# Frequency products rebuilt: sums by accumulating DMAs, mirrored inverse rows, the last W4 groups behind the inverse, and the order as written lists

## The chip, the cores and the metric

One core of a Trainium2 chip runs the kernel. The metric is device time in microseconds (us) of one execution, the median of several runs on the chip. TensorE does the matmuls, ScalarE (ACT) moves results out of PSUM and does the nonlinear functions, VectorE (DVE) does elementwise work in SBUF, GpSimd (POOL) issues some DMAs and does a few tiny operations, SyncE (SP) issues most DMAs.

## The reference

Two branches on the same input `x` (2048 rows, 640 columns, bfloat16), mixed by a gate per row:

```python
x = A_q
g = sigmoid((x * gate_w).sum(-1, keepdims=True))
return g * A(x, A_k, A_v, ...) + (1 - g) * B(x, B_w1, B_w2, B_w3, B_w4)

def A(q, k, v, shift_k, ssm_k, ssm_D):        # long convolution
    k_shift = sum of 4 shifted k, each times a row of shift_k
    kv = k_shift * v
    y = irfft(rfft(pad(kv)) * rfft(pad(ssm_k)))[:2048]     # along the rows, per column
    return q * (y + kv * ssm_D)

def B(x, w1, w2, w3, w4):                     # mixer and MLP
    h = gelu(layernorm(x) @ w1);  hs = (four column groups shifted by 1, -1, 2, -2 rows) @ w2
    x1 = x + hs
    return x1 + gelu(layernorm(x1) @ w3) @ w4
```

## The kernel before

**The operations as nodes.** The Python program makes a list of nodes, one for an engine's operation, with what each reads and writes. `Prog._forward` (from line 210) then plans an order from estimated costs and priorities (`RANK`), and `emit` writes one instruction stream for each engine in that order, with semaphore waits between engines. Each engine works through its stream strictly in order. PSUM is four pairs of banks; a group of matmuls (a job) takes a pair, and the evictions on ScalarE give it back.

**Branch B.** Rows are held as two halves `c` and eight residues `rho` (row = 1024 c + 8 p + rho on partition p). `mm1`, `mm2` (L1075), `mm3` (L1129) and `mm4` (L1147) are its four matmuls. `mm4` goes in four groups `sc` of four row sets; a group's PSUM is first filled with `x1` by ScalarE (`seed`, L1057), then 24 matmuls of 320 columns are added, and one eviction writes the result times `1 - g` back to `X`. All four groups come ahead of the convolution's products in the program; the planner spreads them over the time that VectorE needs.

**Branch A.** The convolution's transform is split: 16 row residues are combined by matmuls with tables of cosines (`forward`, L1178) for two frequency sets `kap` = 0 and 1, on two halves of the columns, for both signals: `h` (the filter taps) and `k` (k times v). Each result, 16 planes of 320 columns, lies in a slot `s0` to `s4`, `t0`, `t1` (or `k0`, `k1`: a column half of `KV`, rows of 640 bytes). For each of the four (half, kap) `unit` then works on VectorE alone, nearly everything through the helper `tt` (L663):
- `butterfly` of `h` and `k`: two instructions of 2560 elements (lower planes plus and minus upper planes) and four of 1280;
- `window`: two of 1280 on `k`;
- `pointwise`: the complex products, six multiplications of 2560, two sums (the first, `pwa`, is an accumulating DMA issued on POOL by `add_dma`, L702; the second is VectorE's) and two last ones (`pwz`);
- `fold`: the way back, two of 2560 and four of 1280.

`inverse` (L1366) makes for each residue `rho` 8 matmuls of 320 columns from both frequency sets; ScalarE evicts them times `g`, VectorE multiplies by q, and adds to `X`: for half 0 by accumulating DMAs (L1392), for half 1 on VectorE, row by row. The last four residues of half 1 are cut into pieces (L1341, L1351) and end the kernel.

**Order around the change.** SP's queue carries the loads, the transposes of the second layer norm, q and the stores; POOL's carries the loads of W3, W4 and the inverse table, the accumulating DMAs and the power instruction of the layer norms (L868).

Of the kernel before, what the change touches and what calls it, by code (L numbers as in the profile page):

```python
# [88 lines left out]
class Prog:  # L89
    LAT = {"pe": (0.0, 0.20), "act": (0.24, 0.16), "dve": (0.12, 0.12), "pool": (0.2, 0.2), "sp": (0.1, 0.1)}  # L90
    LOOK = 1.0

# [86 lines left out]
    PRIO = ()  # L179

    def schedule(self):
        for n in self.nodes:
            n.base = frozenset(n.deps)
        for j in self.jobs:
            own = set(j.nodes)
            j.ext = [d for v in j.nodes if not v.first for d in v.base if d not in own]
            if j.seeded:
                j.nodes[0].soft = [d for v in j.pes for d in v.base if d not in own]
        for n in self.nodes:
            for d in n.deps:  # L190
                d.users.append(n)
        for n in self.nodes:
            n.prio = self.PRIO[n.idx]
        self._forward()

    RATE = 390e3
    WINDOW = 3.4133
    PHASE = 2.4

    def _forward(self):  # L200
        nodes = self.nodes
        for n in nodes:
            n.deps = set(n.base)
            n.missing = len(n.deps)
            n.start = n.end = None
        for j in self.jobs:
            j.pair = None
            j.left = len(j.evicts) if j.evicts else 1
        free = {"pe": 1.0, "act": 0.7, "dve": 0.8, "pool": 1.1, "sp": 0.7}
        ready = {e: [] for e in ENGS}  # L210
        known_at = {}
        pair_free = [0.0] * PAIRS
        pair_job = [None] * PAIRS
        bits = [[False, False] for _ in range(PAIRS)]
        link = 0.0
        xlink = 0.0
        alink = 0.0
        slink = 0.0
        warm = False
        window = -1  # L220
        duty = carry = 0.0
        busy, lock = False, 0.0
        LAT = self.LAT

        def arrive(n):
            at = 0.0
            for d in n.deps:
                t = d.end + (LAT[d.eng][0 if d.eng == n.eng else 1] if d.kind == "c" else 0.05)
                if t > at:
                    at = t  # L230
            known_at[n] = at
            ready[n.eng].append(n)

        for n in nodes:
            if n.missing == 0:
                arrive(n)
        left = len(nodes)
        order = {e: [] for e in ENGS}
        allseq = []
        while left:  # L240
            best = None
            for e in ENGS:
                for n in ready[e]:
                    t = max(known_at[n], free[e])
                    if n.first:
                        j = n.job
                        tp = None
                        for i in range(PAIRS):
                            if pair_job[i] is not None and pair_job[i].left:
                                continue  # L250
                            if j.seeded and not (bits[i][0] and bits[i][1]):
                                continue
                            if tp is None or pair_free[i] < tp:
                                tp = pair_free[i]
                        if tp is None:
                            continue
                        t = max(t, tp)
                        ok = True
                        for d in j.ext:
                            if d.end is None:  # L260
                                ok = False
                                break
                            if not n.seed:
                                t = max(t, d.end - n.cost)
                        if ok and n.seed:
                            for d in n.soft:
                                if d.end is None:
                                    ok = False
                                    break
                                t = max(t, d.end - self.LOOK)  # L270
                        if not ok:
                            continue
                    key = (t, -n.prio, n.idx)
                    if best is None or key < best[0]:
                        best = (key, n)
            assert best is not None, "schedule is stuck"
            n = best[1]
            e = n.eng
            t = best[0][0]
            ready[e].remove(n)  # L280
            n.start = t
            cost = n.cost
            if n.array:
                w = int((t - self.PHASE) // self.WINDOW)
                while window < w:
                    warm = duty > (0.42 if warm else 0.75) * self.WINDOW
                    window += 1
                    duty, carry = carry, 0.0
# [225 lines left out]

def _tables():

# [929 lines left out]
```

## Time and profile before

| | |
|---|---|
| runs | median 225.89 us (225.49 to 226.24, three runs) |
| profiled execution | span 223.5 us from the first to the last instruction; its own time is not listed apart |
| TensorE busy | 216.3 us (97%), 1557 matmuls |
| VectorE busy | 208.7 us (93%), 267 instructions |
| ScalarE busy | 174.6 us (78%) |
| POOL busy | 41.1 us (18%), 48 instructions |
| DMA | 34.04 MB, mean 152 GB/s |

How to read it: spans and windows are in microseconds from the first instruction. A busy share is over the whole span; stages differ. A group row gives the line, engine, operation, shapes and count, then busy time and mean nanoseconds of one, then the idle time of the engine ahead of them with what ended it. A timeline row gives start, length and what ran, merged when the same thing follows itself. A window row gives for each engine its busy time and the number of its instructions, then the TensorE clock granted, the share of the DMA engines and GB/s.

### The profile page before, as it was taken

To read this page: it belongs to the slowest core of one execution; us is meant where nothing else is said; L and a number is where in the kernel's file an instruction comes from. 1 tells how busy PE (TensorE), PEld (TensorE's weight loads), DVE (VectorE), ACT (ScalarE), POOL (GpSimd) and SP (SyncE) were. 2 spreads that over 40 slices of the span, in tenths; PEclk is the share of its full clock that TensorE was granted. 3 is DMA by queue.
4 is the path that set the end of the run, shared out by engine and by line. 5 is a ranking of instruction groups with operands and counts; after the bars stand their busy time and mean duration, and the time that the engine had idled before them with its cause. 6 is when DMAs were issued, how large, how long until landed. Compare 5 with 4: busy or idle time off the path is not lost.

```text
span 223.5 us, 3945 instructions
## 1 busy us (share of the span) xinstructions
PE 216.3 (97%) x1557; PEld 138.0 (62%) x1569; DVE 208.7 (93%) x267; ACT 174.6 (78%) x292; POOL 41.1 (18%) x48
## 2 busy tenths in 40 slices
PE   7999999999999999999999999999999999999993
PEld 7589655557676655457744455667745675577772
DVE  4999899999999899999899999799998999999976
ACT  3989999899999999999987488997145723572484
POOL 1335662403003120450200200000020002033020
PEclk9999999999999999999999999999999999999999
DMA  6999996589801968061654150003559000648667
GB/s 208 385 403 387 350 361 236 116 156 283 349 5 33 345 120 337 4 117 41 126 101 90 24 97 0 1 3 98 137 87 257 11 0 3 117 87 117 151 117 235
DMA packets 36713, 34.04 MB, mean 152 GB/s; under 512 B 17508, under 2 KB 31719, under 8 KB 36568
## 3 DMA queue, kind: packets, MB, share of 16 engines
q1 hardware_dynamic: 31560, 23.97, 35.8%
q0 software_dynamic: 4848, 9.50, 18.9%
q10 hardware_dynamic: 288, 0.33, 0.6%
q8 instruction: 12, 0.20, 0.4%
q14 instruction: 5, 0.04, 0.1%
HBM read 21.47 MB, written 3.93 MB: 114 GB/s over the span
## 4 chain that ended last, share of the span: by engine, by line
PE 76%; ACT 18%; DVE 2%; DMA 2%; issue 1%; SPq 0%; ACTq 0%
PE PS L1147 23%; PE PS L1129 23%; ACT arena L694 12%; PE PS L1178 9%; PE PS L967 8%; PE PS L1366 6%; ACT PS L1057 5%; PE PS L927 2%; ACT arena L680 2%; DVE arena L663 2%; DMA arena<-in_A_q_dram 2%; PE PS L823 1%; PE PS L769 1%; PE PS L758 1%; PE PS L780 0%
## 5 line engine op out<-in xcount | busy, mean ns | idle before, releaser
L663 DVE TENSOR_TENSOR arena<-arena 128x2560 bf16<-128x2560 bf16 (+5 forms) x175 | 186.1, 1116 | 7.0 <-ACT arena L694 3.5
L694 ACT ACTIVATE arena<-PS 128x640 bf16<-128x640 f32 (+8 forms) x142 | 104.2, 812 | 18.9 <-PE PS L1129 14.7
L1147 PE MATMUL PS<-arena 128*128 128x320 bf16 x384 | 53.3, 299 | 0.0
L1129 PE MATMUL PS<-arena 128*128 128x512 bf16 x232 | 52.2, 379 | 0.8 <-ACT arena L694 0.5
L1147 PEld LDWEIGHTS PS<-arena 128*128 128x128 bf16 x384 | 37.4, 98 | 15.0 <-issue 0.3
L694 ACT ACTIVATE arena<-PS,arena 128x320 bf16<-128x320 f32 (+1 forms) x47 | 27.7, 626 | 24.2 <-PE PS L1147 22.2
L1129 PEld LDWEIGHTS PS<-arena 128*128 128x128 bf16 x240 | 23.3, 98 | 27.4 <-issue 0.5
L1178 PE MATMUL PS<-arena 128*128 128x320 bf16 x224 | 34.4, 300 | 0.7 <-DVE arena L906 0.6
L1178 PEld LDWEIGHTS PS<-arena 128*128 128x128 bf16 x224 | 20.8, 98 | 12.8 <-ACT arena L694 2.8
L680 ACT ACTIVATE arena<-arena 128x640 bf16<-128x640 bf16 (+2 forms) x34 | 25.8, 787 | 0.8 <-DMA arena<-in_A_q_dram 0.4
L967 PE MATMUL PS<-arena 128*128 128x512 bf16 (+1 forms) x121 | 22.9, 335 | 0.2
L1075 PE MATMUL PS<-arena 128*128 128x320 bf16 x160 | 22.6, 299 | 0.0
L1057 ACT ACTIVATE PS<-arena 128x640 f32<-128x640 bf16 x32 | 22.3, 719 | 0.2
L868 POOL TENSOR_TENSOR arena<-arena 128x4 f32<-128x4 f32 (+1 forms) x9 | 14.0, 1553 | 30.7 <-DVE arena L668 30.4
L1075 PEld LDWEIGHTS PS<-arena 128*128 128x128 bf16 x160 | 15.4, 98 | 6.7 <-ACT PS L1057 0.6
L967 PEld LDWEIGHTS PS<-arena 128*128 128x128 bf16 x125 | 11.8, 98 | 8.2 <-ACT arena L694 0.5
L702 POOL DMA_DIRECT2D arena<-arena x4 | 4.8, 1202 | 57.6 <-DVE arena L663 57.6
L888 DVE BATCH_NORM_STATS2 arena<-arena 128x6 f32<-128x320 bf16 x28 | 12.4, 477 | 2.9 <-DMA arena<-in_A_q_dram 2.8
L1366 PE MATMUL PS<-arena 128*128 128x320 bf16 x96 | 14.3, 299 | 0.0
L1007 POOL DMA_DIRECT2D arena<-arena x18 | 9.7, 545 | 12.7 <-ACT arena L694 12.7
L1366 PEld LDWEIGHTS PS<-arena 128*128 128x128 bf16 x96 | 9.2, 98 | 4.3 <-issue 0.3
L1392 POOL DMA_DIRECT2D arena<-arena x4 | 5.1, 1276 | 35.7 <-ACT arena L694 25.9
(42 smaller groups left out, 81.5 us busy)
## 6 DMA issues: line engine op xcount, KB each, us to landing
arena<-in_B_w_dram POOLq DMA_DIRECT2D x4, 960.0 KB, 8.2
arena<-in_A_k_dram SPq DMA_DIRECT2D x4, 640.0 KB, 14.3
arena<-in_A_v_dram SPq DMA_DIRECT2D x4, 640.0 KB, 14.1
arena<-arena POOLq DMA_DIRECT2D x4, 640.0 KB, 6.1
arena<-in_A_q_dram SPq DMA_DIRECT2D x4, 640.0 KB, 7.4
out_dram<-arena SPq DMA_DIRECT2D x15, 160.0 KB, 2.0
arena<-in_A_q_dram SPq DMA_DIRECT2D x6, 320.0 KB, 5.5
arena<-in_A_ssm_k_dram SPq DMA_DIRECT2D x3, 512.0 KB, 11.5
```

Of the source, the lines that this page charges most:

```text
L663: return dve(lambda e: e.tensor_tensor(o, a, b, op), [a, b], [o], c_tt(n), tag=tag, **kw)
L680: node = P.op("act", lambda e, ps: e.activation(o, i, func, **kw), r=r, w=[o], cost=c_act(n, naps, acc is not None, psum=False), tag=tag, ...
L694: node = P.op("act", lambda e, ps: e.activation(ov, inner(ps), func, **kw), r=r, w=[o], cost=c_act(n, len(r), acc is not None), job=job, t ...
L868: P.op("pool", lambda e, ps: e.tensor_tensor(r, v, hv, ALU.pow), r=[v, HALF], w=[r], cost=cost, tag="ln")
L888: dve(lambda e, o=o, x=x: e.bn_stats(o, x), [x], [o], 0.393, tag="bn", group=("bn", id(mv), rho, c))
L967: fns.append(lambda e, ps, b=b, c=c, lhsT=lhsT: e.matmul(bank(ps, b, 256 * n), lhsT, XT[:, c, r0:r0 + n, :], start=(c == 0), stop=(c == 4)))
L1057: P.seed(job, lambda e, ps: e.activation(two(ps, 320), x, ACTF.Copy), [X[:, c, rho, :]], c_act(640, psum=False), tag)
L1075: fns.append(lambda e, ps, hh=hh, ft=ft, lhsT=lhsT: e.matmul(bank(ps, hh, 320), lhsT, w2v[:, ft, 320 * hh:320 * hh + 320], start=False, st ...
L1129: fns.append(lambda e, ps, b=b, ft=ft, c=c, sc=sc: e.matmul(bank(ps, b, 512), w3h[ft // 6][:, c, 128 * (ft % 6):128 * (ft % 6) + 128], XT[ ...
L1147: fns.append(lambda e, ps, hh=hh, ft=ft, lhsT=lhsT: e.matmul(bank(ps, hh, 320), lhsT, w4h[ft // 6][:, ft % 6, 320 * hh:320 * hh + 320], st ...
L1178: fns.append(lambda e, ps, w=w, b=b, rhs=rhs, st=(first and n == 0), en=(n == len(ss) - 1): e.matmul(bank(ps, b, 320), w, rhs, start=st, s ...
L1366: fns.append(lambda e, ps, w=w, z=z, c=c, st=(n == 0), en=(n == len(terms) - 1): e.matmul(bank(ps, c, 320), w, z[:, c, :], start=st, stop=en))
```

## The change

The order is no longer planned at build time: `RANK` lists 993 ranks, one for each node, by which the nodes of all engines are sorted, and `PAIR` gives each job its PSUM pair. DMA semaphores are used again by later DMAs.

```diff
+    def schedule(self, rank, pairs):
+        for n in self.nodes:
+            n.prio = rank[n.idx]
+        self.allseq = sorted(self.nodes, key=lambda n: -n.prio)
+        self.order = {e: [n for n in self.allseq if n.eng == e] for e in ENGS}
...
+        for job, pair in zip(self.jobs, pairs):
+            job.pair = pair
```

**Forward.** The second set's odd residues are now built like the even ones: one more table (`FM2` for all four r), two matmuls added onto the first set's sums in the same PSUM pair, and a second eviction. Constant scales 2 and root 2 go into evictions.

```diff
-                if r % 2 == 0:
+                if r % 2 == 0 or (sig, half) in R4M:
...
-                    go(None, lambda s: FM1[:, r // 2, s, ri, :], r, ri, (0, 1), S1_[:, r, ri], True, sig)
+                    go(None, lambda s: FM1[:, r // 2, s, ri, :], r, (0, 1), S1_[:, r, ri], ROOT2, True, sig)
```

**Sums.** `add` makes a sum in place either on VectorE or as an accumulating DMA on POOL, by a set of names:

```diff
+EVEN = (0, 1)
+BY_DMA = {("bh", 0, 0), ("bh", 0, 1), ("bk", 0, 0), ("bk", 0, 1), ("bh", 1, 0), ("bh", 1, 1), ("bk", 1, 0), ("bk", 1, 1),
+          ("pwa", 0, 0), ("pwa", 0, 1), ("pwa", 1, 0), ("pwa", 1, 1), ("fin", 0)}
+BY_DMA = BY_DMA | {("fold", 0, 0), ("fold", 0, 1), ("fold", 1, 0), ("fold", 1, 1), ("mir", 0), ("pwb",0,0),("pwb",0,1),("pwb",1,0)}
+    def add(o, i, n, dma, tag):
+        if dma:
+            add_acc(o, i, n, tag)
+        else:
+            tt(o, o, i, ALU.add, n, tag=tag)
```

**Butterfly, products, fold.** The butterfly makes one difference of 2560 on VectorE and its sum by `add`; the products are made for the difference half (T) and the sum half (S) apart, each with pieces of 1280; `fold` likewise. For `kap` = 1 the butterfly has a turned form with four pieces of 640 and four of 1280.

```diff
+    def butterfly(name, diff, other, turned, dma, tag):
+        tt(D, lo, hi, ALU.subtract, 2560, tag=tag + "d")
+        add(lo, hi, 2560, dma, tag + "a")
...
+        if not turned:
+            tt(Tx[:, 0:4:3], E2, E3, ALU.add, 1280, tag=tag + "t")
+            tt(Tx[:, 2:0:-1], E2, E3, ALU.subtract, 1280, tag=tag + "t")
+            tt(hi[:, 0:4], lo[:, 0:4], lo[:, 4:8], ALU.add, 1280, tag=tag + "s")
+            tt(hi[:, 4:8], lo[:, 0:4], lo[:, 4:8], ALU.subtract, 1280, tag=tag + "s")
+            return T, hi
...
+    def product(H, K, temp0, temp1, da, db, dz, tag):
+        tt(rb[0], kb[0], hb(1, 1), ALU.mult, 1280, tag=tag)
+        tt(tb[1], kb[1], hb(1, 0), ALU.mult, 1280, tag=tag)
+        add(fl(T, 1), fl(R, 0), 1280, da, tag + "a")
+        tt(rb[1], kb[0], hb(0, 1), ALU.mult, 1280, tag=tag)
+        tt(kb[1], kb[1], hb(0, 0), ALU.mult, 1280, tag=tag)
+        add(fl(K, 1), fl(R, 1), 1280, db, tag + "b")
+        tt(tb[0], kb[0], hb(1, 0), ALU.mult, 1280, tag=tag)
+        tt(kb[0], kb[0], hb(0, 0), ALU.mult, 1280, tag=tag)
+        tt(k[:, :, 0], k[:, :, 0], t[:, :, 1], ALU.subtract, 1280, tag=tag + "z")
+        add(k[:, :, 1], t[:, :, 0], 1280, dz, tag + "y")
...
+    def fold(T, S, A, B, dma, tag):
+        tt(E[:, 0:4], S[:, 0:4], S[:, 4:8], ALU.subtract, 1280, tag=tag + "d")
+        tt(E[:, 4:8], T[:, 0:4], T[:, 4:8], ALU.subtract, 1280, tag=tag + "d")
+        add(S[:, 0:4], S[:, 4:8], 1280, dma, tag + "a")
+        add(T[:, 0:4], T[:, 4:8], 1280, dma, tag + "a")
...
```

**Inverse.** For both halves the even residues' two frequency sets are first combined (`mir`: difference on VectorE, sum by `add`), so that an even row takes 4 matmuls in place of 8.

```diff
+        for a in range(2 * (half in EVEN)):
+            x, y = x4[:, a], (y4[:, a] if a == 0 else y4[:, a, ::-1])
+            tt(t4[:, a], x, y, ALU.subtract, 1280, tag=f"mir{a}")
+            add(x, y, 1280, ("mir", half) in BY_DMA, f"mira{a}")
```

**Tail.** The `mm4` group `sc` = 3 (residues 6 and 7) is made last in the program, in two halves of 12 matmuls; its eviction adds the convolution's part, which for those residues is no longer added to `X` beforehand. The cut pieces at the end of the inverse are gone.

```diff
+            elif hhs[0] == 0:
+                x, q = o[:, 0:320], Qh[0][:, c, rho, :]
+                evict(job, x, lambda ps: bank(ps, 0, 320), ACTF.Copy, 320, scale=omg, tag="Bl")
+                tt(x, x, q, ALU.add, 320, tag="finl")
+            else:
+                x, q = o[:, 320:640], Qh[1][:, c, rho, :]
+                P.op("dve", lambda e, ps, x=x, q=q, omg=omg: e.scalar_tensor_tensor(
+                    out=x, in0=bank(ps, 1, 320), scalar=omg, in1=q, op0=ALU.mult, op1=ALU.add),
...
+    units(0, (("bh", 0, "s3", "s0a", "s0b"), ("bk", 0, "s2", "s1a", "s1b"), ("pw", 0, "s1a", "s0a", "s2a", "s3a"),
+              ("bh", 1, "s4", "s0a", "s0b"), ("fold", 0, "s2a", "s1a"), ("bk", 1, "t0", "s1b", "s2b"),
+              ("pw", 1, "s1b", "s0a", "t0a", "s4a"), ("fold", 1, "t0a", "s1b")))
```

598 lines of the change are left out of this document (205 added, 393 removed), and 93 rows, old and new, of tables (PAIR, RANK).

## The prediction

> **What bounds the kernel now.** I read the page's busy times first, then the chain that ended last, then windows and the timeline of VectorE. The busy shares say that two engines are full, not one:
>
> ```profile
> span 223.5 us, 3945 instructions
> PE 216.3 (97%) x1557; PEld 138.0 (62%) x1569; DVE 208.7 (93%) x267; ACT 174.6 (78%) x292; POOL 41.1 (18%) x48
> PE 76%; ACT 18%; DVE 2%; DMA 2%; issue 1%; SPq 0%; ACTq 0%
> ```
>
> The chain names TensorE for 76% of the span. Windows over the stage of the frequency work show how close VectorE is:
>
> ```profile
> core 0: us, PE busy (x) PEld busy (x) DVE busy (x) ACT busy (x) POOL busy (x), PEclk, DMA share, GB/s
> 72.60:212.20 139.60, 138.46 (x882) 84.27 (x891) 134.20 (x144) 101.33 (x160) 17.05 (x13) 1.00 0.44 99
> 69.60:112.00 42.40, 41.22 (x279) 25.26 (x280) 40.41 (x55) 42.28 (x80) 11.36 (x9) 1.00 0.56 149
> ```
>
> In 139.6 us TensorE works 138.5, VectorE 134.2; until 112 us ScalarE is full too (42.28 of 42.40). To gain, work has to leave both TensorE and VectorE. The timelines give the prices and the two ends:
>
> ```profile
> 69.58 3.08 DVE L663 TENSOR_TENSOR arena<-arena 128x2560 bf16<-128x2560 bf16 x2
> 86.18 4.50 DVE L663 TENSOR_TENSOR arena<-arena 128x1280 bf16<-128x1280 bf16 x6
> 92.19 4.29 DVE L663 TENSOR_TENSOR arena<-arena 128x2560 bf16<-128x2560 bf16 x3
> 202.56 9.62 DVE L663 TENSOR_TENSOR arena<-arena 128x2560 bf16<-128x2560 bf16 x9 [0.24 <-DMA arena<-arena]
> 215.83 3.97 PE L1341 MATMUL PS<-arena 128*128 128x320 bf16 x28
> 221.37 0.34 SPq L1356 DMA_DIRECT2D out_dram<-arena  x1
> 221.02 0.33 DVE arena L663
> ```
>
> The pair at 69.58 still belongs to k times v (74 instructions of 2560 elements are 16 of that and 58 of the units; 14 lie before 69.58), so VectorE starts the first unit at 72.6 and ends the last `fold` at 202.56 + 9.62 = 212.18. The last matmul ends at 219.80; the last VectorE instruction ends at 221.35, its store is issued at 221.37, the span ends at 223.5.
>
> Successive VectorE instructions overlap by about 0.09 us: six of 1280 elements in 4.50 are 0.735 each, three of 2560 in 4.29 are 1.40. The pair at 69.58, each on the result before it, took 1.54 each, so following one's own input costs about 0.12. By the same overlap 640 elements cost 0.40:
>
> ```profile
> L663 DVE TENSOR_TENSOR arena<-arena 128x2560 bf16<-128x2560 bf16 x74 | 108.0, 1493 | 3.6 <-ACT arena L694 1.6 <-DMA arena<-arena 1.0
> L663 DVE TENSOR_TENSOR arena<-arena 128x1280 bf16<-128x1280 bf16 x64 | 49.1, 821 | 0.5 <-ACT arena L694 0.2
> L663 DVE TENSOR_TENSOR arena<-arena 128x640 bf16<-128x640 bf16 x8 | 3.8, 489 | 1.4 <-ACT arena L694 1.4
> L1351 DVE SCALAR_TENSOR_TENSOR arena<-PS,arena 128x320 bf16<-128x320 f32 x1 | 0.5, 544 | 0.0
> 195.89 9.78 PE PS L1147 x72
> ```
>
> A matmul of 320 columns is 9.78 / 72 = 0.136.
>
> **The change, part by part. TensorE.** Forward: the 16 odd-row groups of the second frequency set become two matmuls on top of the first set's sums, not four of their own: 32 fewer. Inverse: even rows take two terms, not four: 8 rows, 4 matmuls each, 32 fewer. 64 x 0.136 = 8.7 us, all on an engine that waits for little. The odd-row groups now hold a PSUM pair for a second eviction; even rows did so already, so I count nothing (if pairs run out, up to one eviction, 0.7 us, once or twice). The floor by TensorE: last matmul at 219.8 - 8.7 = 211.1, then 0.2 hand-over, 0.54 for the fused scale-and-add, and from its end to the span's end the 2.15 us that lie there now: 214.0.
>
> **VectorE.** The four units are now 58 instructions of 2560 and 60 of 1280 elements (58 x 1.40 + 60 x 0.735 = 125.3). After: 8 of 2560 (one difference per butterfly), 130 of 1280, 16 of 640 (the turned butterflies), and 6 of 1280 for the mirrors: 11.2 + 100.0 + 6.4 = 117.6. That is 7.7 us less; what leaves with the adds is partly given back by the mirrors and by smaller pieces. `pwz` in both signs and the second sums of unit (1,1) stay.
>
> **The order.** The ranks give one order for all engines; laid beside the 993 operations in the order in which the program creates them, they show that the last mirror add of half 1 stands ahead of 96 matmuls: four inverse rows (24) and six halves of the last W4 groups (72): 96 x 0.136 = 13.1 us, which can't start sooner. What stands beside the big instructions follows from now: the stage's 139.6 us (72.6 to 212.2) hold 58 x 1.40 + 64 x 0.735 = 128.2 of them, so 11.4 are statistics, normalisations, steps on one's own input, and waits. Some 5.6 of that I take to stay (22 small instructions, about 3.1, and 21 steps of 0.12, 2.5); the other 5.8 are waits, which I count anew. So the end by VectorE is 72.6 + 117.6, plus the four products of half 0 (2.9) and one of half 1 (0.4), plus 5.6 = 199.1 at that mirror add; plus 13.1 and 2.9 = 215.1, plus **s**, what VectorE waits in between. The two floors lie 1.1 us apart: s decides.
>
> **The accumulating DMAs** that replace the adds are the unknown. There are eight now; after there are 36: 8 for butterflies (640 KB), 14 for products, 8 for folds, 2 for mirrors (320 KB each), 4 at the end. Their rows:
>
> ```profile
> L702 POOL DMA_DIRECT2D arena<-arena x4: 1177/1196/1238, 94.5 to 196.9; - x4
> DMA to landing us min/median/max: 5.6/6.1/7.0
> L1392 POOL DMA_DIRECT2D arena<-arena x4: 1264/1277/1287, 188.4 to 212.5; - x4
> DMA to landing us min/median/max: 4.5/4.5/6.3
> 97.00:99.00 2.00, 1.97 (x14) 1.03 (x13) 1.97 (x2) 1.91 (x4) 2.00 (x1) 1.00 1.07 193
> 190.50:192.00 1.50, 1.50 (x8) 0.69 (x7) 1.47 (x2) 0.40 (x1) 0.00 (x0) 1.00 1.28 155
> 94.54 1.24 POOL L702 DMA_DIRECT2D arena<-arena  x1
> 69.82 1.73 POOL L706 DMA_DIRECT2D arena<-in_B_w_dram  x2 [17.77 <-DVE arena L663]
> ```
>
> A 640 KB add lands 6.1 us after issue, a 320 KB one 4.5; beside nothing else they stream at 193 GB/s (long rows) and 155 GB/s (rows of 640 bytes, as the products' sums have). So a butterfly's add occupies the queue 3.4 us, a product's 2.1, a fold's 1.7. All of them: 8 x 3.4 + 14 x 2.1 + 10 x 1.7 + about 6 = 80 us of a stage of 127: not the bound by sum, but they queue.
>
> From the list I counted the VectorE work between the instruction that frees each add and the first that needs it. It is 3.6 to 11.0 us, near 6 in most. Against landing time plus 0.2 for the hand-over:
> - `bh` of unit (0,0): 3.6 stand against 6.3: a wait of 2.7. (W3's second half is loaded just ahead of it in the same queue; what it adds, 0 to 2, is in the range.)
> - products of (0,0): four adds come free within 4.6 us and need 8.4 of the queue; the last is some 1.1 late.
> - products of (0,1): 3.9 against 4.7, and queued: 1.3.
> - last fold of (1,1): 3.7 for the second add: 1.0.
> - the first `bk`: 0.2. The others have 0 to 6 us to spare.
>
> That is 6.3. Landings spread by 1 to 2 us (5.6 to 7.0, 4.5 to 6.3), mostly into spare time; ScalarE, full until 112, may hold a window's inputs. For these I count nothing beyond 0.2: **s = 6.5**, a little over the 5.8 of waits now. From below 0 (everything lands in time; less can't be, a list without waits is the floor), from above 16 (21 places wait for such an add; half of them late by one spread of 0.9 is 9.5 more).
>
> POOL issues 28 more times 1.2 us, 34 us on an engine busy for 41; but it is in order: an add that waits for VectorE holds the small power instruction of the second layer norm behind it, and the rows normalised from that. In VectorE's queue, behind a late sum, stand the other signal's window and difference, and POOL's next add waits for those.
>
> Whether POOL's issuing slows VectorE shows at 94.54, where POOL worked 1.24 us:
>
> ```profile
> 93.59 2.89 DVE L663 TENSOR_TENSOR arena<-arena 128x2560 bf16<-128x2560 bf16 x2
> ```
>
> Two in 2.89 is 1.40 each, as elsewhere. So 28 issues cost VectorE 0. The Trainium skill ("SBUF — State Buffer", section "SBUF: two separate sides") says that VectorE and GpSimd lock a shared port pair against each other, also where VectorE has two SBUF inputs and GpSimd reads SBUF. If descriptor writing were caught by it, each issue could stop VectorE for its 1.2 us; the row above does not agree, since nothing slowed.
>
> **Other edits.** 32 evictions get a constant scale. Rows: 735 ns plain, 796 with a scale from memory (behind the window of the loads):
>
> ```profile
> 0.00:22.00 22.00, 20.28 (x238) 16.46 (x239) 17.89 (x64) 17.46 (x30) 7.88 (x15) 1.00 0.94 345
> L694 ACT ACTIVATE arena<-PS 128x640 bf16<-128x640 f32 x84 | 54.7, 735 | 0.1
> L694 ACT ACTIVATE arena<-PS,arena 128x640 bf16<-128x640 f32 x16 | 12.7, 796 | 22.3 <-PE PS L1147 22.2
> ```
>
> At most 32 x 0.06 = 1.9, half of it where ScalarE is full; a constant reads nothing, so I take 0. The forward table grows by 128 KB on SP's queue, 0.4 us at the 345 GB/s of the first 22 us (first row); the second part of it is first used near 30 us, so 0 (up to 0.4 without that cover).
> Stores stay 17, the last of 80 KB as now; five of them move behind the tail's W4 groups, where SP has nothing else to issue. Other semaphores and the order written out cost nothing at run time.
>
> **Sum.** 215.1 + 6.5 = 221.6 against this profiled span of 223.5, so 1.9 less: of 8.7 and 7.7 us of work little is left, since the last 13 us of matmuls follow VectorE's last sum. The median of the runs, 225.89, lies 2.4 above the span; I add the same: **224.0**.
>
> **Rivals.**
> - *The order holds* (s of 3 or less): at s = 2, span 217.1, time 219.5; never below TensorE's 214.0, time 216.4. For it: both floors nearly meet, so the list looks made for it, and spare times stand near the landing times. Against: those were read with one add in flight; after, two to four are. The Trainium skill ("DMA: Bandwidth & Descriptors", section "Anatomy of one DMA — SWDGE (gpsimd) path") fits 2.0 us plus bytes / 436e3; by that every add would land in 3.5 us or less and this rival be the forecast. The rows say 6.1 and 4.5, and they decide.
> - *The adds queue up and the kernel is slower.* One mechanism: the queue is in order, so a late product sum delays the next butterfly's add, whose sums VectorE then waits for, unit after unit. It decides from s = 8.4 on (215.1 + 8.4 = 223.5). At 0.3 us more in each of the 17 places I counted free s is 11.6: span 226.7, time 229.1. For it: landings up to 7.0 and 6.3 with little else moving; the list can't be left when something is late. Against: 80 us of queue in 127, and spare time at most places.
> - *It cancels*: s of 7.7 to 9.1, time 225.2 to 226.6; only 1.2 us of waits away from my sum.
> - *The lock of the two engines*: up to 28 x 1.2 = 34 us more than my sum, 258; nothing in the rows for it.
>
> **Chances.** A measurement tells about 0.3% (0.7 us) from no change. Partly eaten gain, 220.5 to 225.2: 0.40. Order holds, below 220.5: 0.17. Cancels: 0.14. Queue, above 226.6: 0.27. Lock: 0.02. So faster 0.57, same 0.14, slower 0.29. Likeliest 224.0, its own range 220.5 to 225.2; eight in ten need 218.5 (s of 1) to 230.
>
> **What would show it.** Right: about 64 matmuls fewer; VectorE's TENSOR_TENSOR at 2560 down to 24 (with the taps), near 200 us busy; waits of VectorE for DMA between 4 and 8 us in all, the longest near 77 to 81 us; after the last mirror add TensorE without a gap for 13 us and under 3 us behind its last matmul. Wrong: waits for DMA above 9 us (the queue), below 3 (the order holds), instructions of 1280 longer than 0.82 beside POOL's issues (the lock), or TensorE idle in the last 13 us for want of ScalarE's evictions, which I priced at nothing.

## The result, and the profile after

The changed kernel takes **240.03 us** (median; 239.5 to 240.69) against 225.84 us (225.49 to 226.24) for the kernel before on the same chip: ratio 1.063, interval 1.060 to 1.065. The forecast was 224.0 us with a range to 230. The profiled span is 238.7 us, 15.2 above that of before. In the table further down, one run of e2 and one of e5 were over 1.5% longer than the fastest of their kernel: the medians hold them, the ratios leave them out.

The page's busy times, its slices of TensorE and of the granted clock, and its chain that ended last:

```profile
span 238.7 us, 3921 instructions
PE 218.0 (91%) x1501; PEld 134.8 (56%) x1514; DVE 202.1 (85%) x307; ACT 173.8 (73%) x293; POOL 77.1 (32%) x76
PE   6999999999999779998939999999179999999995
PEclk9999999999999999999979999999958999999999
PE 42%; DVE 23%; DMA 18%; ACT 9%; issue 2%; SPq 2%; POOL 2%; DVEq 0%; ACTq 0%
```

The work did shrink: VectorE is busy for 202.1 us, 6.6 less than before. But DMA, 2% of the chain before, is now 18%, and TensorE has holes (slices of 6 us: a 3 near 122 us, a 1 near 170). The transform's matmuls did shrink, to 45.9 us from 53.4; that TensorE is busy 1.7 us more all the same comes mostly from `mm3` (4.2 more for the same work) and from filler matmuls (6.4 more). The view by groups that keeps shapes apart says whose DMA it is:

```profile
L540 DVE TENSOR_TENSOR arena<-arena 128x1280 bf16<-128x1280 bf16 x140 | 106.5, 818 | 12.7 <-DMA arena<-arena 6.8 <-issue 3.6 <-ACT arena L571 2.1
L540 DVE TENSOR_TENSOR arena<-arena 128x2560 bf16<-128x2560 bf16 x24 | 36.3, 1514 | 5.7 <-DMA arena<-arena 5.0
```

And the list of waits (who, for whom: us in total, times, longest):

```profile
DVE arena L540 <- DMA arena<-arena: 11.8, 7, 3.9
DVE arena L540 <- ACT arena L571: 8.9, 7, 2.1
PE PS L1043 <- DMA arena<-arena: 6.6, 1, 6.6
```

VectorE waits 11.8 us for DMAs within SBUF, which are the accumulating sums. That is the forecast's own sign for its rival, "waits for DMA above 9 us (the queue)". TensorE waits once for 6.6 us, at a matmul of `mm3` (L1043), whose input comes from the layer norm's transposes; its hole near 122 us is another wait, of 4.1 us, for ScalarE. DMA rows of the same run (count, size of each, median us to landing):

```profile
arena<-arena POOLq DMA_DIRECT2D x26, 320.0 KB, 5.1
arena<-arena POOLq DMA_DIRECT2D x8, 640.0 KB, 6.2
arena<-arena SPq DMA_TRANSPOSE x16, 6.8
```

The transposes' own line (ns on SP for one issue, min/median/max, then the stretch; below it the landing):

```profile
L979 SPq DMA_TRANSPOSE arena<-arena x16: 1206/1872/4155, 79.3 to 163.0; - x16
DMA to landing us min/median/max: 2.7/6.8/8.6
```

The same transposes in the kernel before:

```profile
L1102 SPq DMA_TRANSPOSE arena<-arena x16: 1199/1270/1284, 74.6 to 119.7; - x16
DMA to landing us min/median/max: 2.6/2.7/4.5
```

A transpose lands after 6.8 us instead of 2.7, and its issue holds SP for up to 4.2 us. Windows of the kernel after (columns as before: busy time of each engine, clock, DMA share, GB/s): the stage from VectorE's first unit to its last mirror sum, then the two stretches around TensorE's hole:

```profile
73.36:221.19 147.83, 132.55 (x804) 76.63 (x810) 126.96 (x189) 100.43 (x164) 53.74 (x43) 0.97 0.94 156
149.00:174.00 25.00, 19.17 (x126) 12.08 (x125) 19.72 (x26) 11.34 (x16) 8.57 (x8) 0.99 1.24 149
174.00:196.00 22.00, 21.12 (x101) 10.68 (x104) 21.21 (x31) 9.37 (x12) 4.32 (x5) 0.86 0.67 130
```

This gives the yardstick for all that follows: **stage length less VectorE's busy time**. Here 147.83 - 126.96 = 20.9 us; before it was 139.6 - 134.2 = 5.4 up to the last fold. Between 149 and 174 us the share of the DMA engines is 1.24 (it adds up packets in flight, so it can pass 1) and VectorE works 19.7 of 25.

### The profile page after: what moved, and what is told of

Its sections match the earlier page's. It is cut to its first block, busy times and chain, and to the rows that moved or that the text cites. A ratio compares the mean times of both kernels' runs of the same rounds, so it can differ in the third digit from the quotient of the medians.

```text
span 238.7 us, 3921 instructions
## 1 busy us (share of the span) xinstructions
PE 218.0 (91%) x1501; PEld 134.8 (56%) x1514; DVE 202.1 (85%) x307; ACT 173.8 (73%) x293; POOL 77.1 (32%) x76
## 4 chain that ended last, share of the span: by engine, by line
PE 42%; DVE 23%; DMA 18%; ACT 9%; issue 2%; SPq 2%; POOL 2%; DVEq 0%; ACTq 0%
DVE arena L540 22%; PE PS L1043 17%; DMA arena<-arena 16%; PE PS L1014 12%; PE PS L1208 5%; ACT arena L571 5%; ACT arena L557 4%; PE PS L844 2%; SPq L979 2%; DMA arena<-in_A_q_dram 2%; PE PS L635 1%; PE PS L804 1%; PE PS L1072 1%; POOL arena L745 1%; POOL arena L884 1%
## 5 line engine op out<-in xcount | busy, mean ns | idle before, releaser
L540 DVE TENSOR_TENSOR arena<-arena 128x1280 bf16<-128x1280 bf16 (+4 forms) x212 | 178.1, 900 | 25.3 <-DMA arena<-arena 11.8
L1093 POOL DMA_DIRECT2D arena<-arena x36 | 42.0, 1214 | 96.0 <-DVE arena L540 95.6
L1043 PE MATMUL PS<-arena 128*128 128x512 bf16 x231 | 56.4, 400 | 12.6 <-DMA arena<-arena 6.6
L1014 PE MATMUL PS<-arena 128*128 128x320 bf16 x384 | 54.2, 299 | 0.9 <-ACT PS L934 0.7
L1043 PEld LDWEIGHTS PS<-arena 128*128 128x128 bf16 x240 | 24.0, 102 | 42.2 <-issue 18.3
L1014 PEld LDWEIGHTS PS<-arena 128*128 128x128 bf16 x384 | 37.1, 98 | 17.0 <-ACT PS L934 1.2
L571 ACT ACTIVATE arena<-PS,arena 128x320 bf16<-128x320 f32 (+1 forms) x48 | 25.8, 593 | 17.2 <-PE PS L1014 9.2
L1072 PE MATMUL PS<-arena 128*128 128x320 bf16 x192 | 31.8, 300 | 0.4
L844 PE MATMUL PS<-arena 128*128 128x512 bf16 (+1 forms) x121 | 24.2, 353 | 0.2
L952 PE MATMUL PS<-arena 128*128 128x320 bf16 x160 | 22.9, 299 | 0.2 <-ACT PS L934 0.2
L1072 PEld LDWEIGHTS PS<-arena 128*128 128x128 bf16 x192 | 16.6, 97 | 10.4 <-ACT arena L571 4.0
L745 POOL TENSOR_TENSOR arena<-arena 128x4 f32<-128x4 f32 (+1 forms) x9 | 16.0, 1778 | 15.6 <-DVE arena L545 12.1
L952 PEld LDWEIGHTS PS<-arena 128*128 128x128 bf16 x160 | 15.3, 98 | 7.0 <-ACT PS L934 0.8
L844 PEld LDWEIGHTS PS<-arena 128*128 128x128 bf16 x125 | 12.7, 104 | 9.1 <-ACT arena L571 0.3
L635 PE MATMUL PS<-arena 128*128 128x128 bf16 x87 | 13.3, 271 | 3.6 <-ACT arena L571 2.4
L1208 PE MATMUL PS<-arena 128*128 128x320 bf16 x96 | 14.1, 299 | 0.0
L884 POOL DMA_DIRECT2D arena<-arena x18 | 9.8, 547 | 10.9 <-ACT arena L571 10.9
L635 PEld LDWEIGHTS PS<-arena 128*128 128x128 bf16 x87 | 8.2, 121 | 8.6 <-ACT arena L571 4.6
(39 smaller groups left out, 76.9 us busy)
## 6 DMA issues: line engine op xcount, KB each, us to landing
arena<-in_A_v_dram SPq DMA_DIRECT2D x4, 640.0 KB, 15.1
```

The source lines that it names most:

```text
L540: return dve(lambda e: e.tensor_tensor(o, a, b, op), [a, b], [o], c_tt(n), tag=tag, **kw)
L571: node = P.op("act", lambda e, ps: e.activation(ov, inner(ps), func, **kw), r=r, w=[o], cost=c_act(n, len(r), acc is not None), job=job, t ...
L635: P.pe([(lambda e, ps: e.matmul(bank(ps, 0, 128), ones, ones, start=True, stop=True)) for _ in range(FILLN)], r=[ones], cols=128 * FILLN, ...
L844: fns.append(lambda e, ps, b=b, c=c, lhsT=lhsT: e.matmul(bank(ps, b, 256 * n), lhsT, XT[:, c, r0:r0 + n, :], start=(c == 0), stop=(c == 4)))
L952: fns.append(lambda e, ps, hh=hh, ft=ft, lhsT=lhsT: e.matmul(bank(ps, hh, 320), lhsT, w2v[:, ft, 320 * hh:320 * hh + 320], start=False, st ...
L1014: fns.append(lambda e, ps, hh=hh, ft=ft, lhsT=lhsT: e.matmul(bank(ps, hh, 320), lhsT, w4h[ft // 6][:, ft % 6, 320 * hh:320 * hh + 320], st ...
```

## The experiments

Theory 1 after the result: the sums by DMA are the cost, through VectorE's waits. Theory 2: the transposes, made late by the sums, stop TensorE and through it everything else. Unless told otherwise each kernel is the changed one with one edit. The next table collects the stage rows; the runs follow one by one. Each ratio is against the kernel before on the same chip, which took 227.07 us on that of e5, e6, e7 and e9 and 225.8 to 226.0 on the others; so spans from different chips compare within about 1 us.

| run | time us | ratio to before (interval) | span | VectorE busy in stage | stage less busy |
|---|---|---|---|---|---|
| after | 240.03 | 1.063 (1.060 to 1.065) | 238.7 | 126.96 | 20.9 |
| e1 sums cut to one plane | 223.96 | 0.9925 (0.9903 to 0.9947) | 221.3 | 126.03 | 5.3 |
| e5 products' sums cut | 230.86 | 1.015 (1.011 to 1.020) | 229.2 | 126.75 | 12.4 |
| e6 the other sums cut | 233.28 | 1.028 (1.023 to 1.034) | 230.2 | 126.39 | 14.5 |
| e7 transposes cut | 233.91 | 1.031 (1.028 to 1.034) | 231.9 | 126.90 | 14.9 |
| e2 transposes earlier | 242.23 | 1.071 (1.065 to 1.077) | 241.3 | 127.35 | 24.8 |
| e3 products' sums on VectorE | 238.73 | 1.058 (1.053 to 1.063) | 237.2 | 136.72 | 10.3 |
| e4 all sums on VectorE | 251.24 | 1.111 (1.107 to 1.115) | 249.3 | 156.77 | 2.4 |
| e12 another order | 239.02 | 1.058 (1.055 to 1.061) | 237.4 | 127.38 | 15.1 |
| e13 other order and choice | 234.54 | 1.037 (1.034 to 1.041) | 234.1 | 130.26 | 9.0 |
| e16 the same, start kept | 227.09 | 1.004 (1.001 to 1.007) | 225.0 | 130.75 | 5.4 |
| e17 second find | 227.06 | 1.004 (1.001 to 1.007) | 224.5 | 130.65 | 3.0 |

**e1: the sums' data taken away, their issues and waits kept.**

```diff
-        return P.dma("pool", lambda e, ps: e.dma_start(o, i, accum_op=ALU.add, ...
+        return P.dma("pool", lambda e, ps: e.dma_start(o[:, 0:1], i[:, 0:1], accum_op=ALU.add, ...
```

> Every accumulating DMA moves only the first plane (or the first half at the end) of what it should add, 82 KB for most in place of 320 or 640; every issue, wait and place in the lists stays. The sums are therefore not the reference's. Theory 1 (the time that the added data needs in the DMA engines is what VectorE and the layer norm's transposes wait for): VectorE's waits fall from 20 us to about 6, the transposes land in about 3 us as before the change, TensorE has no wait of 4.0 and 6.5 us, span 221 to 224, time 224 to 227. Rival (the written order itself, with its couplings between ScalarE, TensorE and VectorE, or the fixed latency of a DMA, costs the time): span stays above 233, time above 235.

Measured: 223.96 us. The stage's window:

```profile
72.57:203.87 131.30, 128.31 (x806) 76.17 (x807) 126.03 (x189) 99.66 (x163) 47.47 (x43) 1.00 0.49 95
```

The DMA rows of the same run:

```profile
arena<-arena POOLq DMA_DIRECT2D x32, 80.0 KB, 2.5
arena<-arena SPq DMA_TRANSPOSE x16, 3.8
```

With the same lists and semaphores, VectorE's idle time falls from 20.9 to 5.3 and 17.4 us of span go. So the loss is the time that the sums' bytes take in the DMA engines, not issuing, not semaphores, not the new instructions. The transposes came to 3.8 us, not quite to the 3 expected. The row also caps the change in this order: with sums that are nearly free it gains 0.75%.

**e2: the last transposes taken earlier,** right behind the statistics of their layer norm group, by new ranks for eight nodes.

> Only the order is changed: the four normalisations and transposes of the second layer norm's last group go directly behind the group's statistics, some 16 us sooner on ScalarE. Theory 2 (the late transposes, 11 us in the DMA engines, hold TensorE and cool its clock, and that alone sets the end): the wait of 6.5 us ahead of the last W3 group and the clock's fall go, span 229, time 231. Theory 1 (VectorE's waits for late sums are right behind): the last mirror add stays near 219, span 234 to 236, time 236 to 238.

Measured: 242.23 us, slower still. TensorE's wait of 6.6 us for the transposes is down to 1.8, but now it stands 6.3 us in front of a forward matmul, for ScalarE. The waits say why nothing was won:

```profile
DVE arena L540 <- ACT arena L571: 12.0, 7, 6.5
DVE arena L540 <- DMA arena<-arena: 10.0, 8, 2.7
PE PS L1072 <- ACT arena L571: 6.3, 1, 6.3
```

The transposes' line names who waited for them:

```profile
  ACT arena L557: 4.5, 2
```

ScalarE normalises the rows into four buffers that it uses again; put earlier, it stood 4.5 us waiting for the transposes to free them. The evictions behind it in its queue came late, and VectorE waited 6.5 us for one, TensorE 6.3. As a test of Theory 2 this run is spoiled by those new waits; e7 asks the same question without it.

**e3 and e4: sums put back on VectorE,** the products' (e3) or all (e4).

```diff
+BY_DMA = {x for x in BY_DMA if x[0] not in ("pwa", "pwb")}      # e3
+BY_DMA = set()                                                  # e4
```

> The 14 sums inside the products go back to VectorE (14 x 0.735 = 10.3 us more work there), the 22 other accumulating DMAs stay. If VectorE's work plus its waits set the end: the waits that hang on these sums (about 11 us of the 15 for DMA) go, so the last mirror add stays within 3 us of 221, span 236 to 241. If the late transposes set the end: with the rows of 640 bytes gone from the queue they land sooner, the wait of 6.5 us shrinks to under 2, span 229 to 233.

> All 36 sums go back to VectorE in the same places of the lists; no accumulating DMA is left. VectorE's busy time rises by 30 us to about 232, its waits for DMA vanish, the transposes land in about 3 us. If the sum of VectorE's work sets the end: span 248 to 254, time 251 to 256. If the DMA traffic was worth more than the work that it saves: span 238 or less.

Measured: 238.73 and 251.24 us. Both spans, 237.2 and 249.3, lie where the first expectation of each put them (VectorE's work plus its waits set the end). e3 gives VectorE 9.8 us more work and takes 10.6 us of idle time away; e4 gives 29.8 more and takes 18.4 away. So taking all sums off VectorE is worth 11 us net in this order, against 30 us of VectorE's work saved. Without any sum by DMA the transposes land as quickly as in the kernel before (e4):

```profile
arena<-arena SPq DMA_TRANSPOSE x16, 2.7
```

**e5 and e6: which sums cost.** The edit of e1 for the products' 14 sums alone, and for all others alone.

> Only the 14 second sums of the products move a seventh or less of their data (the first plane alone); every other accumulating transfer is whole, and lists and waits are those of the changed kernel. The outputs of the products are therefore wrong. With all sums cut the span fell by 17.4 us, to 221.3. Theory A (what counts is the bytes that the sums put into the DMA engines, wherever they stand): the products' sums are a third of the bytes, so a third of the 17.4 us goes: span 232 to 234. Theory B (what counts is the sums with a reader or a reuse directly behind, which are the butterflies' and the folds'; a product's sum has slack): span 237 to 239. Theory C (the jam between 145 and 175 us, where products and transposes meet, is most of it): span 226 to 229.

> The counterpart: the products' 14 second sums are whole, all other accumulating transfers (butterflies, folds, mirror, first output) move only their first plane, so those results are wrong. Theory A (bytes): two thirds of the 17.4 us go, span 226 to 228. Theory B (butterflies and folds alone): span 221 to 223. Theory C (products and transposes): span 232 to 235.

Measured: spans 229.2 and 230.2, 9.5 and 8.5 below the changed kernel; together 18.0, where e1 took 17.4 from both at once. A third of the bytes accounts for half of the loss, so bytes alone are not the measure (A), and the butterflies and folds are not alone to blame (B). Theory C, the jam of products and transposes, comes nearest: these two spans miss its ranges by 0.2 and 1.8 us, and other runs of the same two kernels (228.5 and 228.1; 232.6 and 232.1) lie in them. Within the 1 us or so between chips the two halves add up.

**e7: the transposes taken away.**

```diff
-                x_t = P.dma("sp", lambda e, ps, o=o, b=b: e.dma_start_transpose(o, b), ...
+                x_t = P.dma("sp", lambda e, ps, o=o, b=b: e.dma_start_transpose(o[:, 0:1, :], b[:, 0:128]), ...
```

> The 16 transposes of the second layer norm move 128 of their 640 columns each, so four fifths of the mixer's input in the second half is left out; all sums by transfer are whole. Theory 1 (VectorE's waits for the sums set the end; the transposes are late beside them but on no path that decides): the last mirror sum moves by under 3 us, VectorE's waits stay at 18 to 21 us, span 235 to 238. Theory 2 (sums and transposes slow each other in the same engines): the landing of a transpose falls from 6.8 to 3 us or less, TensorE's wait of 6.5 us ahead of mm3.33 goes, VectorE's waits between 137 and 175 us (9.5 us in sum) fall to 3 or 4, span 230 to 233.

Measured: span 231.9, 6.8 us less and in the range of Theory 2, with all sums whole. The waits:

```profile
DVE arena L540 <- DMA arena<-arena: 9.4, 7, 2.3
DVE arena L540 <- ACT arena L571: 5.5, 6, 1.6
PE PS L1043 <- DMA arena<-arena: 2.4, 2, 2.0
```

The transposes' landing:

```profile
DMA to landing us min/median/max: 3.2/5.5/7.0
```

And the window that follows TensorE's hole in the changed kernel:

```profile
174.00:196.00 22.00, 21.89 (x143) 13.82 (x143) 21.90 (x32) 10.94 (x17) 4.96 (x4) 1.00 0.59 95
```

Theory 1 alone (235 to 238) falls: the transposes have a share in the loss. The sums' median landing is no shorter without them (5.4 and 6.2 us against 5.1 and 6.2); the longest falls from 10.4 to 7.7. The expectation was wrong in one point: a transpose of a fifth of the data still lands only after 5.5 us. So most of its delay is not its own data; with no sums about (e4) the whole transpose lands in 2.7. What went is 2.4 us of VectorE's waits for sums, 3.4 us of its waits for ScalarE, and most of TensorE's hole.

**e9: the order planned anew at build,** by the kernel before's planner with the new ranks as priorities and the traced rates as costs.

> The whole change, with all its transfers at full size, but the order is worked out at build by the planner of the kernel before from the changed kernel's ranks as priorities, with the cost of an accumulating transfer set by the rates that the trace before showed (193 GB/s with long rows, 155 GB/s with rows of 640 bytes). Theory 1 (the loss is the order's: it places readers and reuses as though the sums were quicker): VectorE's waits fall from 21 us to 10 or less and the span comes to 224 to 230. Rival (the loss is the transfers': so many bytes must pass between 75 and 175 us that no order within these buffers hides them): waits stay at 15 us or more, span 234 to 242.

Measured: 253.62 us (ratio 1.118, 1.111 to 1.125), beyond both expectations. VectorE's waits for these DMAs rose to 24.5 us, and TensorE stood 15.2 us before the inverse. The ranks are a finished order and make poor priorities; the run shows only that an order can be much worse, so it does not decide the question.

**e12 and e13: orders found by search.** Many small moves of single operations, judged by a model of five engines and two DMA queues, each in order, with the traces' durations and rates. e12 keeps every transfer; e13 may also choose which sums go by DMA (`BACK` and `TO_DMA` name operation and unit).

```diff
-RANK = [...]; PAIR = [...]
+RANK = [...]; PAIR = [...]          # other lists
     def add(o, i, n, dma, tag):
+        key = f"{tag}:{P.stage}"
+        dma = key in TO_DMA or (dma and key not in BACK)      # e13, e16, e17
```

> The whole change with the same instructions and transfers, all at full size, in another order and with other PSUM pairs: an order found by many small moves in a model of the five engines in order and two DMA queues in order, whose durations and rates are those of the traces. Theory 1 (about half of the loss is the order's: readers and reuses stand too close behind the sums): VectorE's waits fall from 21 to 10 to 13 us and the span comes to 227 to 231; what is left is a chain that no order shortens, since in each of the four units the butterfly's sum, the product's sums and the fold's sums follow one another through VectorE, and the next unit needs their buffers. Theory 2 (all of it is the order's): 221 to 224. Rival (the order doesn't matter, the bytes do): 236 or more.

> Order searched in the same way, and with it which sums go by transfer: eight groups go back to VectorE (one butterfly's sum, six groups of the products, the last fold's) and four real sums of the products go by transfer in their place, so that VectorE's work stays within 4.4 us of the changed kernel's and the sums on each unit's chain cost 0.75 us on VectorE in place of some 6 us of landing. The result is complete. Theory (the chain of sums through each unit is what the transfers lengthen): span 222 to 226, about the kernel before. Rival (what counts is VectorE's work or the bytes, not the place on the chain): the bytes fall by a fifth, VectorE has more to do, span 231 to 236.

Measured: spans 237.4 and 234.1. Both theories missed; the spans lie in the ranges that the rivals gave (236 or more, 231 to 236). The stage windows show whether for the rivals' reason:

```profile
77.50:220.00 142.50, 129.53 (x804) 76.55 (x814) 127.38 (x185) 101.63 (x164) 52.28 (x41) 1.00 0.93 159
```

(that is e12) and

```profile
76.90:216.20 139.30, 131.30 (x805) 77.50 (x815) 130.26 (x191) 101.31 (x166) 42.03 (x35) 0.99 0.83 147
```

(e13). It is not: the idle time fell, to 15.1 us with every byte still moved (e12) and to 9.0 (e13). But both began the first unit late, at 77.5 and 76.9 us against 73.4, because the search had also moved work in the first 70 us.

**e16 and e17: the same search with the first 67 us left alone.** In e16 one butterfly's sum, three folds' (two sums each) and six of the products' go back to VectorE; five others go by DMA.

> As e13, with the order up to 67 us that of the changed kernel, so that the first butterfly begins at 73.4 us as there and not at 76.9. Ten groups of sums go back to VectorE (one butterfly's, three folds', six of the products') and five other sums of the products go by transfer in their place. The result is complete. In e13 VectorE was busy for 130.9 us and waited 8.4 us between the first butterfly and the last mirror sum, and the tail was 18.0 us: with 130 to 131 us busy, 4 to 8 us of waits and a tail of 17.5, 73.4 + 130.5 + 6 + 17.5 gives a span of 227, from 225 to 230. Rival (waits move elsewhere as TensorE now comes late): 231 or more. Under 223.5 would beat the kernel before, and no theory here gives that.

> A second order and choice from the same search: ten groups back on VectorE, of them two folds', five others by transfer. The same sum as for e16_mixed_start: 225 to 230 by the theory, 231 or more by the rival.

Measured: 227.09 and 227.06 us, spans 225.0 and 224.5, at and just below the low end of the expectation: 13 us of the 14 us lost are back. The stage window of e16:

```profile
72.10:208.20 136.10, 130.21 (x805) 76.03 (x815) 130.75 (x195) 100.63 (x162) 51.12 (x32) 1.00 0.82 147
```

Its DMA rows, and VectorE's one wait for a sum:

```profile
arena<-arena POOLq DMA_DIRECT2D x19, 320.0 KB, 4.9
arena<-arena POOLq DMA_DIRECT2D x7, 640.0 KB, 6.3
arena<-arena SPq DMA_TRANSPOSE x16, 2.8
DVE arena L541 <- DMA arena<-arena: 1.0, 1, 1.0
```

A sum takes as long as in the changed kernel (4.9 and 6.3 us, 5.1 and 6.2 there), but VectorE's idle time is 5.4 us instead of 20.9, for 3.8 us more work. And most transposes land after about 2.8 us (the longest takes 6.2). The large sums' rows also carry a fifth fewer bytes (10560 KB against 13440); if the loss went by bytes, an estimate is that a fifth of e1's 17.4 us, 3.7, would be back, not 13. So most of the loss is a matter of place: which sums go by DMA, and what stands between a sum and its reader. How much is the choice and how much the order is not shown; e12, the order alone, took 5.8 us of idle time away and lost 4.1 at the start. No run with the whole computation was faster than the kernel before; e16 is 0.4% slower.

**e10 and e15: what TensorE's saving is worth.** Both are the kernel before with 32 matmuls fewer.

```diff
-                if r % 2 == 0:                                  # e10: all rows by two matmuls
+                if True:
...
-                    go(None, lambda s: FM1[:, r // 2, s, ri, :], r, ri, (0, 1), S1_[:, r, ri], True, sig)   # e15
+                    go(None, lambda s: FM1[:, r // 2, s, ri, :], r, ri, (0,), S1_[:, r, ri], True, sig)
```

> The kernel before with one thing of the change: the odd rows of the second frequency set are taken from the first set's product with two matmuls in place of four, as in the change, but with the second set's weights of the even rows as stand-ins and without the extra turns on VectorE, so the second set's odd rows hold other values. That is 32 matmuls of 0.136 us fewer, 4.35 us of TensorE; VectorE, ScalarE and all transfers do as much as before. Theory (the kernel before stands on both engines at once, and VectorE's list is what TensorE's saving runs into): the span falls by 0 to 1.5 us, 222 to 223.5. Rival (TensorE alone carries the kernel before, as its busy share of 226 in the page suggests): the span falls by 3.5 to 4.5 us, to about 219.5.

> The kernel before, with its own order and PSUM pairs written out as lists, so that no planner runs; the odd rows of the second frequency set sum one of their two terms, two matmuls in place of four, so these rows hold half of their sum. 32 matmuls fewer, 4.35 us of TensorE; everything else is the kernel before. Theory (VectorE's list carries the kernel before from the first butterfly on, so TensorE's saving is worth little by itself): the span falls by 0 to 1.5 us, 222 to 223.5. Rival (TensorE carries it): it falls by 3.5 to 4.5 us, to 219 to 220.

e10: 232.71 us (ratio 1.032, 1.029 to 1.034), slower, outside both expectations. Its planner wrote another order for TensorE and ScalarE, and the odd rows now also hold their PSUM pair for a second eviction (in e15 they don't). VectorE's waits are 15.7 us where they were 7.0, most of them for ScalarE (group rows of e10, then of before); which of the two is the cause was not tried:

```profile
L663 DVE TENSOR_TENSOR arena<-arena 128x2560 bf16<-128x2560 bf16 (+5 forms) x175 | 186.0, 1116 | 15.7 <-ACT arena L694 12.3 <-POOL arena L868 0.9 <-DMA arena<-arena 0.9
```

```profile
L663 DVE TENSOR_TENSOR arena<-arena 128x2560 bf16<-128x2560 bf16 (+5 forms) x175 | 186.1, 1116 | 7.0 <-ACT arena L694 3.5 <-DMA arena<-arena 1.0 <-POOL arena L868 0.9
```

e15 writes the old order out, so that only the matmuls go: 225.87 against 226.04 us, ratio 0.999 (0.997 to 1.002).

```profile
span 223.6 us, 3881 instructions
PE 214.7 (96%) x1525; PEld 134.7 (60%) x1537; DVE 208.4 (93%) x267; ACT 174.1 (78%) x292; POOL 41.3 (18%) x48
```

32 matmuls fewer are worth nothing, although the chain of before put 76% on TensorE: its busy time falls by 1.6 us and the span doesn't.

## Why the prediction was wrong

**Right.**
- The reading that TensorE's saving is not a gain by itself: half of it, taken alone in e15, was worth nothing. That VectorE's list sets the end fits e3 and e4; no run took work off VectorE alone.
- The counts and work: 24 instructions of 2560 left, 202.1 us busy (forecast "near 200"), first unit at 73.4 (72.6).
- The fixed terms of the sum: from the last mirror sum to the end 238.7 - 221.2 = 17.5 us against 16.0, with TensorE without a gap and its last matmul 2.8 us before the end. The 1.5 us more are matmuls of `mm4` that TensorE still had in front.
- POOL's 28 more issues did not slow VectorE: 818 ns for 1280 elements, 821 before. The rule that I weighed there, from the Trainium skill ("SBUF — State Buffer", section "SBUF: two separate sides"), is not seen in this kernel.

**The step that failed** is s, "what VectorE waits in between", taken as 6.5 with bounds 0 and 16. With the forecast's own terms the mirror sum should end at 73.4 + 126.5 = 199.9 plus s; it ended at 221.2, so s was **21.3**. In e1, where the sums move an eighth to a half of their data, the same arithmetic gives 203.9 - 72.6 - 126.5 = 4.8. The outcome of the rival that the forecast gave 0.27, "the adds queue up", came true, at a larger size than its 11.6; its mechanism did so only in part, as the waits show. VectorE's waits for sums on its timeline:

```profile
82.39 8.36 DVE L540 TENSOR_TENSOR arena<-arena 128x1280 bf16<-128x1280 bf16 x11 [2.07 <-DMA arena<-arena]
94.04 1.56 DVE L540 TENSOR_TENSOR arena<-arena 128x1280 bf16<-128x1280 bf16 x2 [0.93 <-DMA arena<-arena]
101.44 3.70 DVE L540 TENSOR_TENSOR arena<-arena 128x2560 bf16<-128x2560 bf16 x4 [1.10 <-DMA arena<-arena]
105.73 1.56 DVE L540 TENSOR_TENSOR arena<-arena 128x1280 bf16<-128x1280 bf16 x2 [0.59 <-DMA arena<-arena]
115.79 4.63 DVE L540 TENSOR_TENSOR arena<-arena 128x1280 bf16<-128x1280 bf16 x6 [1.54 <-issue]
140.18 24.47 DVE L540 TENSOR_TENSOR arena<-arena 128x1280 bf16<-128x1280 bf16 x31 [2.55 <-DMA arena<-arena]
168.56 4.10 DVE L540 TENSOR_TENSOR arena<-arena 128x2560 bf16<-128x2560 bf16 x5 [3.91 <-DMA arena<-arena]
174.72 29.68 DVE L540 TENSOR_TENSOR arena<-arena 128x1280 bf16<-128x1280 bf16 x42 [2.06 <-issue]
205.02 7.57 DVE L540 TENSOR_TENSOR arena<-arena 128x1280 bf16<-128x1280 bf16 x10 [0.62 <-DMA arena<-arena]
```

The view names no releaser for the two waits marked `issue`; by the program's lists the instructions behind them read a fold's and a product's sums, so they count here too. Together that is 15.4 us. At the five places where the forecast counted waits (6.3 us) the rows have 6.1: the butterflies of unit (0,0) 2.1 and 0.9, the products of (0,0) 0.6 and of (0,1) 2.6, the last fold none. The other 9.2 us stand at places counted as free, and 5.1 more are waits for ScalarE and POOL inside the stage. After the first unit no wait is for a butterfly's sum, which the rival had named. What was missing in the working:

- *The buffers that a sum reads.* I counted only readers of a sum's result. A sum also holds its source until it has landed. The longest of VectorE's waits (168.56) is of this kind: a butterfly's difference (2560 elements) is written over the source of products' sums. It stands in unit (1,1); the same happens in unit (0,1), at 101.44 us, and the two make 5.0 us.
- *The transposes.* In the kernel before they run from 74.6 to 119.7 us with eight sums in the whole kernel; I priced their sharing of the DMA engines at nothing. e7 puts it at 6.8 us of span, part of it through TensorE, over which the chain that ended last runs from 174.8 us on.
- *The spread.* I put late landings at 0.2 us because most would fall into spare time. e5 and e6 show the two groups costing 9.5 and 8.5 us, and the waits stand all along the stage. That one late sum shifts the next one's issue, as the rival said, is likely from the lists but not shown by itself. All 36 sums together land in 3.2 to 10.4 us, where the forecast's rows had 4.5 to 7.0 us.

The landing times themselves were near in the median (5.1 us against 4.5 for 320 KB, 6.2 against 6.1 for 640). The formula of the Trainium skill that I set beside them ("DMA: Bandwidth & Descriptors", section "Anatomy of one DMA — SWDGE (gpsimd) path"), 2.0 us plus bytes / 436e3, gives an estimate of 2.2 us for the 80 KB sums of e1, which landed in 2.5; for 320 KB it gives 2.75 where 5.1 were measured. It fits small sums here and not large ones.

What stays open: how much of the 21 us is each sum's own lateness and how much is passed on from the one before. e5 to e7 remove whole groups, and their effects (9.5, 8.5, 6.8) overlap.

## What to carry to other kernels

When sums leave an engine for a DMA queue, count for each one the time until its result is read *and* until its source is written again, and ask what else is in the DMA engines in that stretch; a queue that was summed up as 80 us of work in 127 still set the pace. Ask first which engine's list sets the end: 32 matmuls fewer on an engine that the chain named for 76% of the span were worth 0.0%. Edits that go through a planner change the order too, so write the old order out before measuring one of them alone.

## What the runs showed of the hardware

- Transposes by DMA beside accumulating DMAs: landing 6.8 us instead of 2.7, issue on SP up to 4.2 us instead of 1.3. Cutting their data to a fifth left 5.5 us (e7); with small sums it was 3.8 (e1), without sums 2.7 (e4), and with another order and choice of sums 2.8 (e16).
- A sum by DMA of 80 KB lands in 2.5 us, of 320 KB in about 5, of 640 KB in 6.2: far from proportional.
- Behind TensorE's 6.6 us hole the granted clock was 0.86 for 22 us (row 174.00:196.00 of after); in e7, where that hole is 2.0 us, it was 1.00 in the same stretch. Whether the hole is the cause was not tried by itself. The chain that ended last has this stretch on TensorE:

```profile
174.82 13.45 PE PS L1043 x49
205.26 4.26 PE PS L1043 x19
```

  That is 0.274 us for a matmul behind the hole and 0.224 for the same kind later, at clock 1.00, so by an estimate from these rows the lower clock added 2.5 us to that chain.
